# A feed-forward kernel in float32 halves: sums of weights spread over two steps, block 2 of the first layer in the order of blocks 0 and 1, and ScalarE's order at the turn of layers

## The chip, the cores and the metric

The kernel runs on one core of one Trainium2 chip. The metric is the device time of one execution in microseconds (us); a profiled execution gives the rows below. Engines are named as in the profile: PE (TensorE's matmuls), PEld (its weight loads), DVE (VectorE), ACT (ScalarE), POOL (GpSimd), SP (the queue that issues the transfers).

## The reference

Channel attention over 6016 tokens of 256 channels, and then two feed-forward layers of 2048 hidden columns, each with weights of its own:

```python
x = (v @ a).reshape(6016, 256)     # a: softmax of normalized k^T q, 256x256
h = x @ w_in                       # layer 1: 256 -> 2048
x = (h - np.tanh(h)) @ w_out       #          2048 -> 256
h = x @ w2_in                      # layer 2, the same sizes
g = np.where(h > 0.0, h, np.exp(np.minimum(h, 0.0)) - 1.0)
return g @ w2_out
```

The weights of both layers come as 64-bit numbers, which the kernel turns into float32 itself.

## The kernel before

**Products in halves.** Every operand of a matmul is split into a high and a low part (`ghi`/`glo`, `vhi`/`vlo`, `win` with `win_hi` and `win_lo`, `wout`), and a product is three matmuls: high by high, low by high, high by low. The split is a copy into the matmul's type on ACT (high) and a subtraction on DVE or POOL (low).

**Blocks and steps.** The tokens are cut into 12 blocks `b` of 512 columns (the last has 384), the hidden columns into 8 pairs of 128, `p`. The code counts layers from 0. A step `(layer, b, p)` makes `h` of one pair (12 matmuls of 512 columns into PSUM, `emit_h`, L270), applies the activation (ACT's tanh, DVE's `g = h - tanh`, ACT's `ghi`, the low part `glo`), and some steps later adds the pair's share of the output `o` (12 matmuls, `emit_out`, L869). `LAG` is that distance: `pend` holds the steps whose `o` is still to come.

**Seven products instead of eight.** From block 3 of the first layer on, odd steps with `p` in `PAIRS` = (1, 3, 5, 7) go through `emit_h7`: 21 matmuls of 256 columns (lines L672 to L674, PSUM tiles `q`), for which sums of the four weight blocks are needed (`wsum`, four tiles per pair and a high and low part) and sums of the four parts of the activations (`t`, `thi`, `tlo`, by `sum_v`). The results are put together on ACT and DVE into `hs` (L681 to L691).

**Sums of weights.** `own_sums(p)` makes `wsum` of the first layer: one addition of the two parts of `win` (`whole`, L627, 128x512), four sums of 128x128 (L612), a cast on ACT (L618), the low part (L619). Before, all of it but the cast is on POOL, and it is called after steps 1, 3, 5 and 7 of block 2. For the second layer `sums_of` runs in `conv.store()`, from two tiles `cut` of the converter, and writes to DRAM (`sums_dram`).

**The converter.** The class `Converter` turns the second layer's weights into parts in 32 units while the first layer runs. A unit passes through `load` (a transfer), `first` (two ACT instructions, L113 and L114), `second` (four DVE instructions, L130, L136, L142 and L149, which leave the tile `cut`), `third_scalar` (ACT, L190), `third_pool` (POOL, L197) and `store` (a transfer to DRAM). `nlow` and `ncut` are the numbers of buffers of two of its tiles; both are 3 for the late converter. Steps that go through `emit_h7` run no part of it. In block 11 the finished weights are loaded back over the first layer's.

**Order.** All of it is written out by hand, under a manual schedule, and each engine takes its instructions in that order. Blocks 0 and 1 run first, their steps interleaved, through `emit_act`, with `LAG` 2: tanh, `g`, the converter's parts, `ghi`, `glo`. All other blocks run through the class `Act` with `LAG` 3, in which `ghi` and `glo` of a step are issued in the step after:

```python
act = Act(layer, b, p, h[2][:, :, : blocks[b][1]])   # tanh, or exp and tanh
...
elif before and layer == 0:
    before.lower()                                   # glo of the step before
...
for fill in second:                                  # the converter on DVE
    fill()
conv.store()
...
act.begin()                                          # g = h - tanh
```

**PSUM.** Up to block 2, `h` has two buffers (pool `ps_h`). At block 3 this pool closes, `ps_q` opens in its place for the tiles `q`, and the `h` of even steps gets the one buffer of `ps_b`. So a `q` of block 3 cannot start before DVE has read both last `h` of block 2, and from then on each `h` waits for DVE's `g` of the even step before. `emit_evac` copies a finished `o` out of PSUM on ACT (`osb`, L886), after which the next block's `o` may start.

Of the kernel before, what the change touches and what calls it, by code (L numbers as in the profile page):

```python
# [8 lines left out]
F32 = mybir.dt.float32  # L9
# [3 lines left out]
ALU = mybir.AluOpType  # L13
# [9 lines left out]
def kernel(  # L23
# [488 lines left out]
    with tc.manual_schedule():  # L512
# [92 lines left out]
        def halves(x):  # L605
            return x.rearrange("p c (h t) -> p (c h) t", h=2)

        def sums_of(p, first, second, away):
# [25 lines left out]
        def sum_v(i, raw):  # L634

            x = halves(raw)
            t = steady[0].tile([P, 4, width // 2], F32, tag="t", name=f"t{i}")
            tt = nc.vector.tensor_tensor
            tt(out=t[:, 0:4:2], in0=x[:, 1:4:2], in1=x[:, 0:2], op=ALU.subtract)
            tt(out=t[:, 1], in0=x[:, 3], in1=t[:, 0], op=ALU.subtract)  # L640
            tt(out=t[:, 3], in0=x[:, 2], in1=t[:, 1], op=ALU.subtract)
            hi = steady[0].tile([P, 4, width // 2], F32R, tag="thi", name=f"thi{i}", bufs=2)
            nc.scalar.activation(out=hi, in_=t, func=AF.Copy)
            t_of[i] = (t, hi)
# [87 lines left out]

        def emit_act(layer, b, p, h, fold, late=False, full=False):
            _, n = blocks[b]
# [4 lines left out]
            def between():  # L739

                conv.third_scalar()
                conv.third_pool()
                conv.load()
                conv.first()


            second = conv.second()

# [26 lines left out]
            if layer == 0:  # L775
# [8 lines left out]
                between()  # L784
                nc.scalar.activation(out=hi, in_=g, func=AF.Copy)
            else:

# [133 lines left out]
        for s, (layer, b, p) in list(enumerate(order))[3 : 2 * NP]:  # L921
            if conv is early and early.done() and s >= starts[-1]:
                right.close()
                steady.append(ctx.enter_context(tc.tile_pool(name="steady", bufs=1, side="right")))
                wsum = steady[0].tile([P, 2, len(PAIRS), 4, P], F32R, name="wsum")
                conv = Converter(late_stack, "l", NU // 2, late_units, 3, 1, 3, 3)
                conv.load()
# [15 lines left out]
            if s == 2 * NP - 2:  # L943
                split_v(nv)
                nv += 1

        LAG = 3
        before = None
        for s, (layer, b, p) in list(enumerate(order))[2 * NP :]:
            if conv.done() and not conv.ready and not late_pool:  # L950
                late_stack.close()
# [39 lines left out]
            else:  # L991
                second = conv.second()
                if before and not before.apart and layer == 0:
                    before.upper()
                act = Act(layer, b, p, h[2][:, :, : blocks[b][1]])
                if before and before.apart:
                    before.begin()
                    before.end()
                    before.upper()
                    before.lower()  # L1000
                elif before and layer == 0:
                    before.lower()
                elif before:
                    before.upper()
                    before.lower()
                if done:
# [14 lines left out]
            if nv < len(phases):  # L1021
                if p == 0:
                    load_v(nv)
                    raw = v_of[nv]
                if p == 2:
                    split_v_scalar(nv)
                if p == 3:
                    split_v_rest(nv, nc.vector)
                apart = strassen(*phases[nv], PAIRS[0])
                if p == 5 and apart:  # L1030
                    sum_v(nv, raw)
                if p == 7:
                    if apart:
                        sum_v_rest(nv, nc.vector)
                    nv += 1
        before.upper()
# [40 lines left out]
```

## Time and profile before

| | us |
|---|---|
| median of 3 runs | 1056.19 (1054.81 to 1056.95) |
| the profiled execution | 1056.99 |
| its span, first to last instruction | 1055.0 |
| PE busy | 1024.9 (97%) |
| DVE busy | 883.0 (84%) |
| ACT busy | 680.7 (65%) |
| POOL busy | 284.7 (27%) |

A busy share is a mean over stages. The profile also has, for each engine, what an instruction waited for (the releaser) and how long, the busy times within any stretch of the span with TensorE's granted clock (1.00 is 2.4 GHz, 0.50 is 1.2 GHz), and the order in time. Times of rows count from the first instruction.

### The profile page before, as it was taken

The page shows a single profiled execution, that of the slowest core. Times are in us where ns is not written, and L with a number is a line of the kernel's source. Part 1 is how long each engine was busy: PE and PEld are TensorE (multiplying, and loading weights), DVE is VectorE, ACT ScalarE, POOL GpSimd, SP SyncE. Part 2 cuts the span into 40 slices and gives each one's busy share as a digit, 9 for nine tenths or more (in the row PEclk, how much of TensorE's full clock was granted, in tenths as well). Part 3 has the DMA queues.
Part 4 walks back from the last instruction along what each step waited for, and adds up shares of the span by engine and source line. Part 5 has one row for each costly group of instructions (what it writes and reads, how often), then busy time and mean ns, then how long its engine had stood idle before and what let it go on. Part 6 is the DMA issues. An engine that isn't in the chain of part 4 may idle for free.

```text
span 1055.0 us, 14543 instructions
## 1 busy us (share of the span) xinstructions
PE 1024.9 (97%) x5638; PEld 922.1 (87%) x5638; DVE 883.0 (84%) x1063; ACT 680.7 (65%) x850; POOL 284.7 (27%) x185
## 2 busy tenths in 40 slices
PE   9999997799999999999999999999999999999998
PEld 8888886689788798889999889989899899998998
DVE  7899978896979879777556889899889889889875
ACT  7887675565556565555544676766766667676664
POOL 4522225333323332322210212222122221221210
PEclk9999999899999999999999999999999999999999
DMA  9733123222223121110067100100100000000000
GB/s 357 271 100 100 51 80 110 90 91 80 90 70 97 64 90 51 71 51 16 21 218 225 52 21 21 40 21 21 41 21 21 24 37 21 21 28 28 21 10 27
DMA packets 49253, 75.65 MB, mean 72 GB/s; under 512 B 3360, under 2 KB 25120, under 8 KB 49184
## 3 DMA queue, kind: packets, MB, share of 16 engines
q1 hardware_dynamic: 48896, 74.20, 20.8%
q8 instruction: 44, 0.72, 0.3%
q10 hardware_dynamic: 288, 0.52, 0.1%
q14 instruction: 25, 0.20, 0.1%
HBM read 51.91 MB, written 22.81 MB: 71 GB/s over the span
## 4 chain that ended last, share of the span: by engine, by line
PE 71%; DVE 6%; ACT 3%; issue 1%; POOL 1%; DVEq 0%; ACTq 0%
PE o L869 35%; PE h L270 20%; PE q L673 5%; PE q L672 5%; PE q L674 5%; DVE g L716 2%; PE o_last L869 1%; DVE glo L729 1%; ACT osb L886 1%; ACT ghi L725 1%; POOL glo L729 1%; DVE vlo L250 1%; POOL sum L612 0%; DVE cut L142 0%; ACT vhi L243 0%
## 5 line engine op out<-in xcount | busy, mean ns | idle before, releaser
L869 PE MATMUL o<-ghi,wout 128*128 128x512 f32 (+1 forms) x1472 | 347.0, 379 | 2.5 <-ACT osb L886 2.4
L729 POOL TENSOR_TENSOR glo<-g,ghi 128x1024 fp32r<-128x1024 f32 x76 | 182.9, 2407 | 605.9 <-ACT ghi L725 482.1
L869 PEld LDWEIGHTS o<-ghi,wout 128*128 128x128 f32 x1472 | 272.0, 190 | 37.3 <-ACT osb L886 3.6
L270 PE MATMUL h<-vhi,win 128*128 128x512 f32 (+1 forms) x900 | 282.9, 376 | 14.8 <-DVE g L716 14.0
L725 ACT ACTIVATE ghi<-g 128x1024 fp32r<-128x1024 f32 (+1 forms) x175 | 182.4, 1042 | 87.1 <-DVE g L720 51.7
L270 PEld LDWEIGHTS h<-vhi,win 128*128 128x128 f32 x900 | 170.1, 190 | 41.0 <-DVE g L716 18.4
L869 PE MATMUL o<-glo,wout 128*128 128x512 f32 (+1 forms) x736 | 187.2, 377 | 0.0
L270 PE MATMUL h<-vlo,win 128*128 128x512 f32 (+1 forms) x450 | 168.5, 375 | 0.0
L869 PEld LDWEIGHTS o<-glo,wout 128*128 128x128 f32 x736 | 138.5, 189 | 18.9
L729 DVE TENSOR_TENSOR glo<-g,ghi 128x1024 fp32r<-128x1024 f32 (+1 forms) x99 | 119.0, 1202 | 36.6 <-ACT ghi L725 36.6
L712 DVE SCALAR_TENSOR_TENSOR g<-e,g 128x1024 f32<-128x1024 f32 (+1 forms) x95 | 114.2, 1202 | 23.5 <-ACT g L706 23.1
L270 PEld LDWEIGHTS h<-vlo,win 128*128 128x128 f32 x450 | 85.8, 191 | 10.6
L705 ACT ACTIVATE e<-hs 128x1024 f32<-128x1024 f32 x44 | 46.6, 1059 | 67.5 <-DVE hs L691 67.5
L684 DVE TENSOR_TENSOR hs<-q,hs 128x512 f32<-128x512 f32 x76 | 52.2, 687 | 38.0 <-ACT hs L681 30.1
L716 DVE TENSOR_TENSOR g<-h,g 128x1024 f32<-128x1024 f32 (+1 forms) x48 | 56.3, 1174 | 18.7 <-ACT g L702 18.7
L705 ACT ACTIVATE e<-h 128x1024 f32<-128x1024 f32 (+1 forms) x51 | 50.6, 992 | 32.7 <-PE h L270 32.6
L702 ACT ACTIVATE g<-h 128x1024 f32<-128x1024 f32 (+1 forms) x48 | 47.3, 985 | 34.7 <-PE h L270 33.9
L702 ACT ACTIVATE g<-hs 128x1024 f32<-128x1024 f32 x32 | 33.9, 1059 | 55.1 <-DVE hs L691 53.4
L720 DVE SCALAR_TENSOR_TENSOR g<-g,h 128x1024 f32<-128x1024 f32 (+1 forms) x51 | 60.4, 1185 | 5.7 <-DVE g L712 0.5
L673 PE MATMUL q<-tlo,wsum 128*128 128x256 f32 x228 | 63.2, 277 | 0.0
L672 PE MATMUL q<-thi,wsum 128*128 128x256 f32 x228 | 63.1, 277 | 0.0
L674 PE MATMUL q<-thi,wsum 128*128 128x256 f32 x228 | 63.0, 276 | 0.0
(179 smaller groups left out, 1753.6 us busy)
## 6 DMA issues: line engine op xcount, KB each, us to landing
qk<-in_q_dram SPq DMA_DIRECT2D x23, 256.0 KB, 5.0
vraw<-in_vT_dram SPq DMA_DIRECT2D x11, 512.0 KB, 4.0
x<-osb SPq DMA_DIRECT2D x11, 512.0 KB, 2.7
vraw<-x SPq DMA_DIRECT2D x11, 512.0 KB, 3.2
out_dram<-osb SPq DMA_DIRECT2D x11, 512.0 KB, 2.7
qk<-in_k_dram SPq DMA_DIRECT2D x21, 256.0 KB, 5.2
raw0in<-in_moe_w_in_dram SPq DMA_DIRECT2D x8, 512.0 KB, 3.8
raw0out<-in_moe_w_out_dram SPq DMA_DIRECT2D x8, 512.0 KB, 3.6
```

The lines of the kernel that those rows point to most:

```text
L270: nc.tensor.matmul(out=out, lhsT=w, rhs=x, start=(i == 0), stop=(i == len(pairs) - 1))
L672: nc.tensor.matmul(out=out, lhsT=weights[0], rhs=hi, start=first, stop=False)
L673: nc.tensor.matmul(out=out, lhsT=weights[0], rhs=lo, start=False, stop=False)
L674: nc.tensor.matmul(out=out, lhsT=weights[1], rhs=hi, start=False, stop=end)
L702: nc.scalar.activation(out=self.g, in_=h, func=AF.Tanh)
L705: nc.scalar.activation(out=self.e, in_=h, func=AF.Exp)
L712: nc.vector.scalar_tensor_tensor(out=self.g, in0=self.e, scalar=1.0, in1=self.g, op0=ALU.add, op1=ALU.mult)
L716: nc.vector.tensor_tensor(out=self.g, in0=self.h, in1=self.g, op=ALU.subtract)
L720: nc.vector.scalar_tensor_tensor(out=self.g, in0=self.g, scalar=0.0, in1=self.h, op0=ALU.min, op1=ALU.max)
L725: nc.scalar.activation(out=self.hi, in_=self.g, func=AF.Copy)
L729: engine.tensor_tensor(out=self.lo, in0=self.g, in1=self.hi.bitcast(F32), op=ALU.subtract)
L869: nc.tensor.matmul(out=columns(o[c][:, :n]), lhsT=w[:, f, c * P : (c + 1) * P], rhs=turned(x[:, i]), start=(f == 0 and w is wout_hi and x ...
```

## The change

Five things change:

- Block 2 of the first layer gets a loop of its own: `emit_act` and a `LAG` of 2, as for blocks 0 and 1. In it the converter runs in step 0 alone (`convert=p == 0`); its other seven units of that block move to later steps.
- `own_sums` runs on DVE, after steps 1, 2, 4 and 6. Its cast is issued behind the step's evacuation, and its low part in the next step (`sums_left`).
- For the second layer, POOL's four sums stay in `conv.store()`, and the cast, the low part and the transfer are issued in the converter's next step.
- The late converter has four buffers `cut` instead of three.
- At the turn of layers two ACT instructions change places: `ghi` of the last step of block 11 comes before the exp of the second layer's first step, and in step (1, 0, 2) the evacuation of block 11 comes before `ghi`.

```diff
-            sub = lambda o, a, b, op=ALU.subtract: nc.gpsimd.tensor_tensor(out=t[:, o], in0=a, in1=b, op=op)
+            engine = nc.gpsimd if away else nc.vector
+            sub = lambda o, a, b, op=ALU.subtract: engine.tensor_tensor(out=t[:, o], in0=a, in1=b, op=op)
...
-            nc.scalar.activation(out=dest[:, 0], in_=t, func=AF.Copy)
-            nc.gpsimd.tensor_tensor(out=dest[:, 1], in0=t, in1=dest[:, 0].bitcast(F32), op=ALU.subtract)
-            if away:
-                nc.sync.dma_start(out=sums_dram[j], in_=dest.bitcast(F32))
+            def cast():
+                nc.scalar.activation(out=dest[:, 0], in_=t, func=AF.Copy)
+
+            def low():
+                engine.tensor_tensor(out=dest[:, 1], in0=t, in1=dest[:, 0].bitcast(F32), op=ALU.subtract)
+                if away:
+                    nc.sync.dma_start(out=sums_dram[j], in_=dest.bitcast(F32))
+
+            sums_left.append((cast, low))
...
-            nc.gpsimd.tensor_tensor(
+            nc.vector.tensor_tensor(
                 out=a, in0=win_hi[:, :, fs].bitcast(F32), in1=win_lo[:, :, fs].bitcast(F32), op=ALU.add
...
                 nc.scalar.activation(out=hi, in_=g, func=AF.Copy)
+                for extra in work:
+                    extra()
...
-                conv = Converter(late_stack, "l", NU // 2, late_units, 3, 1, 3, 3)
+                conv = Converter(late_stack, "l", NU // 2, late_units, 3, 1, 3, 4)
...
+        OWN = (1, 2, 4, 6)
+        for s, (layer, b, p) in list(enumerate(order))[2 * NP : 3 * NP]:
+            h = emit_h(layer, b, p)
+            done = pend.pop(0)
+            emit_out(*done)
+            work = []
+            if p == 3:
+                work.append(lambda: split_v_rest(nv, nc.vector))
+            if p == 5:
+                work.append(lambda: sum_v(nv, raw_of[0]))
+            if p == 7:
+                work.append(lambda: sum_v_rest(nv, nc.vector))
+            if sums_left:
+                cast, low = sums_left.pop()
+                work.append(low)
+            if p in OWN:
+                work.append(lambda: own_sums(PAIRS[OWN.index(p)]))
+            pend.append((layer, b, p, emit_act(layer, b, p, h, None, convert=p == 0, work=work)))
+            emit_evac(*done[:3])
+            if sums_left:
+                sums_left[0][0]()
...
-        for s, (layer, b, p) in list(enumerate(order))[2 * NP :]:
+        for s, (layer, b, p) in list(enumerate(order))[3 * NP :]:
...
-                if before and not before.apart and layer == 0:
+                if before and not before.apart and before.layer == 0:
                     before.upper()
                 act = Act(layer, b, p, h[2][:, :, : blocks[b][1]])
                 if before and before.apart:
                     before.begin()
                     before.end()
+                    if (layer, b, p) == (1, 0, 2):
+                        emit_evac(*done[:3])
                     before.upper()
                     before.lower()
-                elif before and layer == 0:
+                elif before and before.layer == 0:
                     before.lower()
...
                 for fill in second:
                     fill()
+                if sums_left:
+                    for part in sums_left.pop():
+                        part()
                 conv.store()
...
-            if layer == 0 and b == 2 and p % 2 == 1:
-                own_sums(PAIRS[p // 2])
```

What else was at the end of the loop (loading and splitting the next block's input) became the function `prepare`, in the same order.

The first place is DVE in block 2 of the first layer, from step 4's `glo` of the step before to step 5's `g` (`h_2_4` is `h` of block 2, step 4; `hz` and `cut` are the converter's). Before:

```order
L729 TENSOR_TENSOR glo<-g,ghi 128x1024
L130 SCALAR_TENSOR_TENSOR hz<-sq,raw1in_1561 128x256
L136 TENSOR_SCALAR cut<-hz 128x256
L142 SCALAR_TENSOR_TENSOR cut<-hz,cut 128x256
L149 ISA cut<-cut,low 128x512
L716 TENSOR_TENSOR g<-h_2_4_1691,g 128x1024
```

In the change the same stretch, from step 4's `g` to step 5's, reads:

```order
L793 TENSOR_TENSOR g<-h_2_4_1657,g 128x1024
L636 TENSOR_TENSOR whole<-win 128x512
L615 TENSOR_TENSOR sum<-whole 128x128 x2
L615 TENSOR_TENSOR sum<-sum,whole 128x128
L615 TENSOR_TENSOR sum<-whole,sum 128x128
L770 TENSOR_TENSOR glo<-g,ghi 128x1024
L793 TENSOR_TENSOR g<-h_2_5_1697,g 128x1024
```

The four instructions of the converter ahead of `g` are gone, five of the sums stand behind `g`, and `glo` now belongs to the same step.

The second place is POOL in block 4, around the second layer's first sums of that block (`out` is the low part of a converted unit). Before:

```order
L729 TENSOR_TENSOR glo<-g,ghi 128x1024
L612 TENSOR_TENSOR sum<-cut 128x128 x2
L612 TENSOR_TENSOR sum<-sum,cut 128x128
L612 TENSOR_TENSOR sum<-cut,sum 128x128
L619 TENSOR_TENSOR sums_out<-sum,sums_out 128x512
L197 TENSOR_TENSOR out<-cut,out 128x256
```

In the change:

```order
L742 TENSOR_TENSOR glo<-g,ghi 128x1024
L615 TENSOR_TENSOR sum<-cut 128x128 x2
L615 TENSOR_TENSOR sum<-sum,cut 128x128
L615 TENSOR_TENSOR sum<-cut,sum 128x128
L197 TENSOR_TENSOR out<-cut,out 128x256
L742 TENSOR_TENSOR glo<-g,ghi 128x1024
L626 TENSOR_TENSOR sums_out<-sum,sums_out 128x512
```

The low part moved behind the `glo` of the converter's next step, and ACT's cast, which it waits for, moved with it.

The third place is ACT at the turn of layers, from the tanh of the last step of block 11 to the evacuation `osb` of that block. Before:

```order
L702 ACTIVATE g<-h_11_7_5345 128x2x384
L705 ACTIVATE e<-h_0_0_5385 128x1024
L706 ACTIVATE g<-h_0_0_5385 128x1024
L725 ACTIVATE ghi<-g 128x2x384
L681 ACTIVATE hs<-q_1_0_1_5423 128x256
L725 ACTIVATE ghi<-g 128x1024
L705 ACTIVATE e<-hs 128x1024
L706 ACTIVATE g<-hs 128x1024
L705 ACTIVATE e<-h_0_2_5475 128x1024
L706 ACTIVATE g<-h_0_2_5475 128x1024
L725 ACTIVATE ghi<-g 128x1024
L886 ACTIVATE osb<-o_11_5214 128x2x12x16 x2
```

In the change:

```order
L715 ACTIVATE g<-h_11_7_5345 128x2x384
L738 ACTIVATE ghi<-g 128x2x384
L718 ACTIVATE e<-h_0_0_5385 128x1024
L719 ACTIVATE g<-h_0_0_5385 128x1024
L694 ACTIVATE hs<-q_1_0_1_5423 128x256
L738 ACTIVATE ghi<-g 128x1024
L718 ACTIVATE e<-hs 128x1024
L719 ACTIVATE g<-hs 128x1024
L718 ACTIVATE e<-h_0_2_5475 128x1024
L719 ACTIVATE g<-h_0_2_5475 128x1024
L904 ACTIVATE osb<-o_11_5214 128x2x12x16 x2
L738 ACTIVATE ghi<-g 128x1024
```

The 384-column `ghi` moved ahead of the second layer's first exp, and `osb` ahead of the last `ghi` shown.

## Rows read from the trace of the kernel before

**Rows 1.** Waits of PE from 100 us on: total us, times, longest.

```profile
PE h L270 <- DVE g L716: 14.0, 9, 2.4
PE q L672 <- DVE g L716: 6.0, 1, 6.0
PE o L869 <- ACT osb L886: 2.4, 1, 2.4
```

**Rows 2.** Windows by block: us; busy (count) PE, PEld, DVE, ACT, POOL; clock; DMA.

```profile
139.54:185.78 46.24, 39.92 (x182) 33.70 (x180) 34.08 (x45) 28.41 (x43) 20.74 (x28) 1.00 0.34 109
185.78:234.63 48.85, 42.85 (x229) 38.06 (x228) 44.83 (x61) 30.09 (x46) 18.34 (x16) 0.93 0.29 92
234.63:279.47 44.84, 42.42 (x229) 37.70 (x228) 33.56 (x49) 26.01 (x37) 15.39 (x13) 0.96 0.25 83
279.47:320.40 40.93, 40.73 (x230) 36.52 (x229) 33.83 (x47) 25.43 (x36) 11.82 (x7) 1.00 0.24 77
320.40:365.71 45.31, 42.85 (x229) 37.66 (x228) 39.42 (x52) 26.21 (x38) 16.60 (x15) 0.96 0.26 82
...
406.64:450.28 43.64, 41.18 (x230) 36.51 (x228) 37.13 (x47) 24.76 (x34) 15.63 (x14) 1.00 0.18 61
450.28:490.74 40.46, 40.46 (x230) 36.60 (x228) 29.29 (x37) 22.48 (x25) 10.48 (x6) 1.00 0.14 43
...
564.66:607.60 42.94, 40.57 (x230) 36.79 (x230) 34.38 (x40) 25.90 (x30) 7.23 (x3) 0.96 0.30 97
```

**Rows 3.** The chain that ended last, one piece: start us, us.

```profile
244.91 2.59 PE h L270 x12
```

**Rows 4.** Timeline at the end of block 2 and in block 3: start us, us.

```profile
180.60 0.63 ACT L618 ACTIVATE wsum<-sum 128x512 fp32r<-128x512 f32 x1 [3.05 <-POOL sum L612]
197.09 0.58 PE L672 MATMUL q<-vhi,win 128*128 128x256 f32 x1 [5.97 <-DVE g L716]
```

**Rows 5.** Timeline in block 4, step 4: DVE, ACT, PE.

```profile
264.72 0.53 DVE L136 TENSOR_SCALAR cut<-hz 128x256 uint32<-128x256 uint32 x1 [4.03 <-POOL sum L612]
265.67 0.63 ACT L618 ACTIVATE sums_out<-sum 128x512 fp32r<-128x512 f32 x1 [4.24 <-POOL sum L612]
267.56 0.48 PE L270 MATMUL h<-vhi,win 128*128 128x512 f32 x1 [2.42 <-DVE g L716]
```

**Rows 6.** Timeline in block 5: DVE twice, POOL once.

```profile
306.35 2.64 DVE L149 CUSTOM_DVE_ANT_0 cut<-cut,low 128x512 uint16<-128x512 uint16 x1
317.56 0.42 DVE L149 CUSTOM_DVE_ANT_0 cut<-cut,low 128x512 uint16<-128x512 uint16 x1
306.33 2.37 POOL L729 TENSOR_TENSOR glo<-g,ghi 128x1024 fp32r<-128x1024 f32 x1 [8.31 <-ACT ghi L725]
```

**Rows 7.** Timeline at the turn of layers: ACT three times, PE once.

```profile
569.27 0.84 ACT L725 ACTIVATE ghi<-g 128x768 fp32r<-128x768 f32 x1
580.61 1.06 ACT L725 ACTIVATE ghi<-g 128x1024 fp32r<-128x1024 f32 x1 [0.72 <-DVE g L720]
581.58 1.51 ACT L886 ACTIVATE osb<-o 128x384 f32<-128x384 f32 x2
583.14 3.52 PE L869 MATMUL o<-ghi,wout 128*128 128x512 f32 x8 [2.37 <-ACT osb L886]
```

**Rows 8.** Groups of instructions by line: busy us, mean ns, idle before.

```profile
L729 DVE TENSOR_TENSOR glo<-g,ghi 128x1024 fp32r<-128x1024 f32 x84 | 103.3, 1230 | 12.4 <-ACT ghi L725 12.4
L716 DVE TENSOR_TENSOR g<-h,g 128x1024 f32<-128x1024 f32 x40 | 48.7, 1218 | 14.1 <-ACT g L702 14.1
L639 DVE TENSOR_TENSOR t<-vraw 128x512 f32<-128x512 f32 x19 | 13.1, 688 | 0.0
L640 DVE TENSOR_TENSOR t<-vraw,t 128x256 f32<-128x256 f32 x19 | 8.1, 425 | 0.7
L627 POOL TENSOR_TENSOR whole<-win 128x512 f32<-128x512 f32 x4 | 5.2, 1304 | 0.0
L612 POOL TENSOR_TENSOR sum<-whole 128x128 f32<-128x128 f32 x8 | 4.2, 546 | 0.3
```

More of the change, by code (lines that the diff above doesn't have):

```diff
@@ L606, in halves @@
             return x.rearrange("p c (h t) -> p (c h) t", h=2)
+        sums_left = []
         def sums_of(p, first, second, away):
@@ L641, in sum_v, with sum_v_scalar @@
             tt(out=t[:, 3], in0=x[:, 2], in1=t[:, 1], op=ALU.subtract)
+            t_of[i] = t
+        def sum_v_scalar(i):
+            t = t_of[i]
             hi = steady[0].tile([P, 4, width // 2], F32R, tag="thi", name=f"thi{i}", bufs=2)
@@ L731, with emit_act @@
         lower = []
-        def emit_act(layer, b, p, h, fold, late=False, full=False):
+        def emit_act(layer, b, p, h, fold, late=False, full=False, convert=True, work=()):
             _, n = blocks[b]
@@ L739, in between @@
             def between():
+                if not convert:
+                    return
+                conv.store()
                 conv.third_scalar()
@@ L744, in between @@
                 conv.first()
-            second = conv.second()
+            second = conv.second() if convert else []
             def fill(i):
@@ L945, with prepare @@
                 nv += 1
+        def prepare(p):
+            nonlocal nv
+            if nv == len(phases):
+                return
+            apart = strassen(*phases[nv], PAIRS[0])
+            if p == 0:
+                load_v(nv)
+                raw_of[0] = v_of[nv]
+            if p == 2:
+                split_v_scalar(nv)
+            if p == 3:
+                split_v_rest(nv, nc.vector)
+            if p == 5 and apart:
+                sum_v(nv, raw_of[0])
+                sum_v_scalar(nv)
+            if p == 7:
+                if apart:
+                    sum_v_rest(nv, nc.vector)
+                nv += 1
+        raw_of = [None]
+        OWN = (1, 2, 4, 6)
[4 more added lines that the diff above has]
+            work = []
+            if p == 3:
+                work.append(lambda: split_v_rest(nv, nc.vector))
+            if p == 5:
+                work.append(lambda: sum_v(nv, raw_of[0]))
+            if p == 7:
+                work.append(lambda: sum_v_rest(nv, nc.vector))
[8 more added lines that the diff above has]
+                sums_left[0][0]()
+            if p == 0:
+                load_v(nv)
+                raw_of[0] = v_of[nv]
+            if p == 2:
+                split_v_scalar(nv)
+            if p == 5:
+                sum_v_scalar(nv)
+            if p == 7:
+                nv += 1
         LAG = 3
         before = None
-        for s, (layer, b, p) in list(enumerate(order))[2 * NP :]:
-            if conv.done() and not conv.ready and not late_pool:
+        for s, (layer, b, p) in list(enumerate(order))[3 * NP :]:
+            if conv.done() and not conv.ready and not sums_left and not late_pool:
                 late_stack.close()
@@ L1005 @@
                     before.lower()
-                if done:
+                if done and (layer, b, p) != (1, 0, 2):
                     emit_evac(*done[:3])
@@ L1018 @@
             pend.append((layer, b, p, (act.hi, act.lo)))
-            if layer == 0 and b == 2 and p % 2 == 1:
-                own_sums(PAIRS[p // 2])
[L1021 to L1035, printed above, removed]
+            prepare(p)
         before.upper()
```

## The prediction

> **What bounds the kernel now.** The page comes first: PE is busy for 97% of the span, so time can only be won where PE waits or runs at the lower clock. Next comes the list of PE's waits behind the attention part [rows 1]: 14.0 us in nine waits of `h` for DVE's `g`, 6.0 us in one wait of `q` for the same, and 2.4 us in one wait of `o` for ACT's `osb`. The windows by block show where they lie and what they cost in all [rows 2]. A block in which PE never waits takes 40.46 us (block 9, and block 10 is the same to 0.01 us): eight `o`, four `h` and four `q`. One `h` or one `o` is 12 matmuls and takes 2.59 us [rows 3].
>
> So block 2, eight `h` and seven `o` in its window, would take 15 x 2.59 = 38.85 us and takes 46.24: 7.39 lost. Against 40.46, block 3 loses 8.39, block 4 4.38, block 5 0.47, block 6 4.85, block 7 again 0.47 (its row is like block 5's), block 8 3.18. Together 29.13 us. The first block of the second layer has three `o` of 384 columns in place of 512, so its floor is 40.46 - 3 x 2.59 x 0.25 = 38.52 us; it takes 42.94 and loses 4.42. That is more than the 22.4 us of waits: the granted clock's mean is 0.93 in block 3 and 0.96 in blocks 4, 6 and the turn, so a part of each ran at 1.2 in place of 2.4 GHz, behind a pause of 2.4 us or more [rows 2, 4, 5, 7]. Block 8 has the pause and a clock of 1.00, and loses some 1.2 to 1.7 us less than blocks 4 and 6: a fall does not follow each such pause.
>
> **Block 2 and the way into block 3.** Before, DVE computes `g` behind the converter's four instructions, and ACT stands in front of `wsum`'s cast until POOL has made the sums: 3.05 us for the third pair, and much the same for the other three [rows 4]. Tanh, `g`, `ghi` and `glo` of a step hang on one another, the delay adds up from step to step, and at the end `q` finds the last `h` unread: 5.97 us [rows 4].
>
> The change takes seven units of the converter out of this block and POOL's work too. What DVE gets for it: for each pair one `whole` of 128x512, four sums of 128x128, one low part of 128x512, spread over two steps. A DVE instruction of 128x512 takes 0.69 us, one of 128x256 0.43 [rows 8]; one of 128x128 is not shown on DVE. Bounds: 0.21 (half of the 256-column one) and 0.55 (POOL's own 128x128 sum); I take 0.30, nearer DVE's row, since part of an instruction is fixed: from 512 to 256 columns only 0.26 of 0.69 goes. Two steps, 4 and 5, the fullest: two `g` and two `glo`, 2 x (1.22 + 1.23) = 4.90; sums 0.69 + 1.20 + 0.69 = 2.58; the three instructions for `t`, 0.69 + 2 x 0.43 = 1.55. Sum 9.03 us, in the 10.36 us that PE needs for two steps of 5.18. At POOL's prices (1.30, 4 x 0.55, 1.30) it would be 11.2 and cost at most 0.9 us in each of four pairs, 3.5 us in all; I take nothing, and keep 3.5 for the range.
>
> The waits that are added: the cast stands on ACT behind `g` and the sums, and the next tanh behind it. In steps 1 and 2, with the two `osb` or `vhi` on ACT as well, I expect a tanh 1 to 2 us late. It is covered: `h` has two buffers, so the `h` two steps on starts 3 x 2.59 = 7.77 us after this one's end, and tanh and `g` need some 2.3. `glo` now stands behind the sums on DVE; with a `LAG` of 2 its `o` comes four pieces, 10.36 us, after the end of `h`, and the chain up to `glo` is about 6. The first `q` of block 3 starts one `o` and one `h`, 5.18 us, behind the last `h` of block 2, and tanh and `g` of that step are done after about 2.3. So block 2 should run at PE's pace, and both of its losses go, 7.39 and nearly all of block 3's 8.39.
>
> **The second layer's sums.** In block 4 DVE's L136 waits 4.03 us for POOL's sums, which free the tile `cut` that it writes, ACT's cast waits 4.24 us for them, and PE's next `h` 2.42 [rows 5]. It happens three times: in blocks 4, 6 and 8. With the fourth `cut` the sums that a unit has to await are those of the converter's step before, about 10 us old; the cast and the low part come another step later and find their inputs ready. These waits go.
>
> What stays is what blocks 5 and 7 show, 0.47 us each. There L149 takes 2.64 us in place of 0.42, from the start of POOL's `glo` to its end [rows 6]: DVE stands still beside POOL, `g` is late, and `h` with it. The seven units that left block 2 now run in blocks 8 to 10, four to a block, so blocks 9 and 10 get this loss too. I put 0.47 on blocks 3, 5, 7 and 9, and 0.7 on blocks 4, 6, 8 and 10, which have the sums on top (block 4 lost nothing before its sum; the cast is 0.63 us of ACT): 4.7 us. Bounds: nothing, and twice 0.47 in all eight blocks, 7.5.
>
> The Trainium skill (SBUF — State Buffer, section "SBUF: two separate sides") says that VectorE and GpSimd share a port pair which one instruction holds alone, and that the other "fully blocks". The 2.64 beside 2.37 us agrees. It speaks against this change as far as converter steps move to blocks that had none: were the whole block of 2.2 us to reach PE in the seven moved steps, they would cost 15.5 us where the rows of blocks 5 and 7 say 0.12 a step, 0.8.
>
> **The turn of layers.** `o` of the second layer waits 2.37 us for block 11's evacuation, which takes 1.51 us and stands behind a `ghi` that itself waited 0.72 us [rows 7]. Put ahead of that `ghi`, with nothing else moved, it would run from 579.89 to 581.40 and end 1.69 us sooner: 0.7 of the wait would be left. The 384-column `ghi` of 0.84 us, which stood between the second layer's first tanh and the next `hs`, moves to where ACT was idle, and DVE's `glo` behind it; that takes most of the rest. I take 0.1 left and no fall of the clock: 4.3 of 4.42. Bounds: 1.7 (only the step above) and 4.4. The `ghi` now behind `osb` is wanted by an `o` two pieces later, over 5 us, which covers 1.5.
>
> **Sum.** 29.13 - 4.7 + 4.3 = 28.7 us. The profiled execution took 1056.99 us (1055.0 from first to last instruction, 2.0 around it), 0.8 over the median of 1056.19. So 1028.3 by the one and 1027.5 by the other: I say **1028 us**.
>
> **Rivals.**
> The sums go on stalling: the cast or L136 still waits for POOL, only elsewhere. For it: POOL's order keeps `glo`, of 2.4 us, ahead of the sums. Against: a whole converter step now lies between. Blocks 4, 6 and 8 lose 11.0 over what block 5 loses, 3.7 each; in four blocks 14.7 in place of the 0.9 put there: 1042 us.
>
> DVE goes on setting block 2's pace. For it: the sums are new work on DVE, and ACT's cast waits for DVE in the same step. Against: 9.0 of 10.36 us. With 7.4 kept, 1035; with block 3's wait kept as well, 1043.
>
> The turn keeps its wait, since something else, such as `hs`, is what makes `osb` late: 1028 + 4.3 = 1032 us.
>
> Slower: the standstill of DVE beside POOL reaches PE. Place: L149 in the 32 converter steps of blocks 3 to 10. Price: up to 2.22 us each. What the change can win without these steps is 29.13 + 4.3 = 33.4 us, so it decides from 1.04 us a step on; at the full price 71 us come in and 33.4 go out, 1094 us. For it: `glo` and L149 start together [rows 6], and the sums follow on POOL. Against: in blocks 5 and 7 the same standstill left 0.12 us a step, since the `h` that waits for `g` has an `o`, a `q` and an `o` before it.
>
> **How the numbers follow.** Forecast 0.64 (its own range 1024 to 1032, from the bounds of the residue and of the turn); the turn kept 0.12; the sums stall 0.10; DVE paces block 2 0.11, half of it on either side of 1037; slower 0.03. Below, no more can go than all 33.5: 1022.6. The range from 1023 to 1037 leaves out the stalling sums, half of the DVE case and the slower one, 0.18. A measurement of this kernel tells 0.2%, 2 us, from no change; all cases but the last are well past it, and 0.01 is left for no change: faster 0.96, same 0.01, slower 0.03.
>
> **What would show it.** In the profile after, the list of PE's waits should have no wait over 1 us between 100 us and the turn, none of `q` for `g`, and none or a short one of `o` for `osb`. The window of block 2 should be 8 x 5.18 = 41.4 us, the next one, with one `o` less, 38 to 38.5, blocks 4 to 10 between 40.5 and 41.4, and the clock 1.00 in all. L136 and the casts should wait for no sum; L149 should still have calls of 2.6 us, now up to block 10. I am wrong if block 2 takes over 43 us, if an even block takes over 42, or if blocks 9 and 10 show a new wait of PE.

## The result, and the profile after

The changed kernel takes 1027.49 us (median of 4 runs, 1027.16 to 1029.13) against 1055.5 of the kernel before in the same set of runs; the ratio is 0.974, 95% interval [0.9718, 0.9761]. In a second set of runs, on another chip, it took 1029.70 and the kernel before 1055.12: 0.9762 [0.9745, 0.9778]. The forecast was 1028. The profiled execution took 1027.36 us, its span is 1025.6 (before 1055.0), PE is busy for 99% of it, and the granted clock is 1.00 throughout.

The waits of PE from 100 us on, in the changed kernel (line, releaser: us in total, times, longest):

```profile
PE h L270 <- DVE g L729: 1.4, 7, 0.2
PE o L887 <- ACT osb L911: 0.2, 1, 0.2
```

Of the 22.4 us in [rows 1] 1.6 are left, and no wait is over 0.21 us. The windows by block, which answer to [rows 2] (us; busy PE, PEld, DVE, ACT, POOL; clock; DMA): blocks 2, 3, 4, 5, 9 and 10, and the first two blocks of the second layer.

```profile
139.59:181.03 41.44, 41.44 (x193) 36.29 (x192) 32.78 (x52) 26.25 (x32) 0.74 (x1) 1.00 0.17 58
181.03:219.38 38.35, 38.16 (x218) 34.26 (x217) 32.85 (x46) 24.39 (x35) 9.30 (x6) 1.00 0.24 76
219.38:260.79 41.41, 41.17 (x229) 36.51 (x228) 39.50 (x49) 26.13 (x38) 15.79 (x14) 1.00 0.27 90
260.79:301.72 40.93, 40.72 (x229) 36.52 (x228) 35.19 (x49) 25.61 (x37) 12.80 (x9) 1.00 0.24 77
...
424.52:465.46 40.94, 40.73 (x230) 36.52 (x229) 35.19 (x49) 25.62 (x37) 12.81 (x9) 1.00 0.22 71
465.46:505.92 40.46, 40.46 (x230) 36.60 (x229) 31.72 (x42) 23.45 (x31) 16.85 (x14) 1.00 0.18 62
539.36:577.90 38.54, 38.54 (x230) 35.65 (x229) 33.00 (x38) 25.90 (x30) 7.24 (x3) 1.00 0.33 110
577.90:618.81 40.91, 40.73 (x229) 36.67 (x228) 37.08 (x43) 27.68 (x32) 9.57 (x4) 1.00 0.07 27
```

The sixteen pieces of block 2 take 16 x 2.59 us and PE never stops in them. Block 3 has no wait of `q` any more. Blocks 6, 7 and 8 (left out) are 40.93 to 40.94 as block 5 is, where they had been 45.31, 40.93 and 43.64. The last row shows a new loss: the second layer's second block took 40.45 before (607.60 to 648.05) and now takes 40.91.

The window of the two fullest steps of block 2 on DVE, from one `g` to the `g` two steps on:

```profile
164.31:174.58 10.27, 8.35 (x14) 1.00 0.01 2
```

DVE is busy for 8.35 of 10.27 us. The price that was missing, a sum of 128x128 on DVE, and the casts on ACT in that block (busy us and mean ns of the group; then start and us of the rows, with the wait and its releaser in brackets):

```profile
L615 DVE TENSOR_TENSOR sum<-whole 128x128 f32<-128x128 f32 x8 | 2.0, 288 | 0.1
```

```profile
157.77 0.63 ACT L623 ACTIVATE wsum<-sum 128x512 fp32r<-128x512 f32 x1 [1.20 <-DVE sum L615]
158.31 1.05 ACT L243 ACTIVATE vhi<-vraw 128x1024 fp32r<-128x1024 f32 x1
159.26 1.01 ACT L792 ACTIVATE g<-h 128x1024 f32<-128x1024 f32 x1
163.16 1.02 ACT L792 ACTIVATE g<-h 128x1024 f32<-128x1024 f32 x1 [0.55 <-PE h L270]
```

The cast waits 1.20 us at most, in place of 3.05. At PE's pace of 5.18 us a step, counted back from the tanh at 163.16, the tanh behind this cast and `vhi` would start at 157.98; it starts at 159.26, 1.3 us late, and the one behind the cast before it 0.4 us late. The tanh at 163.16 already waits for PE again, so the delay is used up within a step.

The second layer's sums in block 4 of the changed kernel, which answer to [rows 5] (timeline of all engines, rows of ACT, POOL, DVE and PE):

```profile
246.55 0.61 ACT L623 ACTIVATE sums_out<-sum 128x512 fp32r<-128x512 f32 x1
...
246.73 2.38 POOL L742 TENSOR_TENSOR glo<-g,ghi 128x1024 fp32r<-128x1024 f32 x1 [6.12 <-ACT ghi L738]
246.80 2.58 DVE L149 CUSTOM_DVE_ANT_0 cut<-cut,low 128x512 uint16<-128x512 uint16 x1
249.06 1.46 POOL L626 TENSOR_TENSOR sums_out<-sum,sums_out 128x512 fp32r<-128x512 f32 x1
249.31 1.21 DVE L729 TENSOR_TENSOR g<-h,g 128x1024 f32<-128x1024 f32 x1
...
250.57 0.48 PE L270 MATMUL h<-vhi,win 128*128 128x512 f32 x1 [0.21 <-DVE g L729]
```

The cast waits for nothing. What is late here is `g`, and it is late by L149, which began 0.07 us behind POOL's `glo` and ended 0.27 us behind it: 2.58 us in place of 0.42. The wait of PE that it leaves is 0.21 us, but the block loses 0.47 by it: from `h` to `h` PE needs 10.12 us, this one starts 10.48 behind the one at 240.09, and its first matmul takes 0.48 us in place of 0.38. The other 0.48 us of block 4 is lost in its first steps, where an `o` starts late behind the evacuation `osb` (the weight load of that `o`):

```profile
237.39 1.59 PEld L887 LDWEIGHTS o<-ghi,wout 128*128 128x128 f32 x8 [0.22 <-ACT osb L904]
```

Two calls of L149 stood ahead of it, at 225.73 and 235.61 (2.65 and 2.61 us).

The turn of layers, on ACT:

```profile
551.98 1.01 ACT L719 ACTIVATE g<-h 128x1024 f32<-128x1024 f32 x1
552.94 1.58 ACT L904 ACTIVATE osb<-o 128x384 f32<-128x384 f32 x2
554.28 1.10 ACT L738 ACTIVATE ghi<-g 128x1024 fp32r<-128x1024 f32 x1
```

The evacuation starts right behind the tanh ahead of it, is over at 554.52, and the `o` that needs it starts at 555.08 without a wait; [rows 7] had 2.37.

### The profile page after: what moved, and what is told of

It reads as the page before. It is cut to its first block, busy times and chain, and to the rows that moved or that the text cites. A ratio compares the mean times of both kernels' runs of the same rounds, so it can differ in the third digit from the quotient of the medians.

```text
span 1025.6 us, 14532 instructions
## 1 busy us (share of the span) xinstructions
PE 1016.4 (99%) x5638; PEld 917.7 (89%) x5638; DVE 883.5 (86%) x1087; ACT 680.5 (66%) x850; POOL 266.6 (26%) x161
## 4 chain that ended last, share of the span: by engine, by line
PE 82%; DVE 10%; ACT 4%; issue 3%; DVEq 0%; ACTq 0%
PE o L887 38%; PE h L270 24%; PE q L687 4%; PE q L686 4%; PE q L685 4%; PE S L338 4%; DVE g L729 2%; PE o_last L887 1%; ACT osb L904 1%; DVE glo L742 1%; DVE vlo L250 1%; PE aw L270 1%; DVE hs L700 1%; DVE hs L697 1%; DVE g L725 1%
## 5 line engine op out<-in xcount | busy, mean ns | idle before, releaser
L738 ACT ACTIVATE ghi<-g 128x1024 fp32r<-128x1024 f32 (+1 forms) x167 | 173.8, 1041 | 99.2 <-DVE g L733 51.4
L742 DVE TENSOR_TENSOR glo<-g,ghi 128x1024 fp32r<-128x1024 f32 (+1 forms) x91 | 108.0, 1187 | 20.1 <-ACT ghi L738 20.1
L270 PEld LDWEIGHTS h<-vlo,win 128*128 128x128 f32 x450 | 85.1, 189 | 10.3
L697 DVE TENSOR_TENSOR hs<-q,hs 128x512 f32<-128x512 f32 x76 | 52.1, 686 | 40.7 <-ACT hs L694 39.3
L700 DVE TENSOR_TENSOR hs<-q,hs 128x512 f32<-128x512 f32 x76 | 52.6, 692 | 8.3 <-DVE hs L697 0.5
L733 DVE SCALAR_TENSOR_TENSOR g<-g,hs 128x1024 f32<-128x1024 f32 x44 | 53.9, 1225 | 1.5
```

The lines of the kernel that those rows point to most:

```text
L270: nc.tensor.matmul(out=out, lhsT=w, rhs=x, start=(i == 0), stop=(i == len(pairs) - 1))
L697: tt(out=hs[:, 0:8:4], in0=quads(q62), in1=two(3), op=ALU.add)
L700: tt(out=hs[:, 1:3], in0=quads(q57), in1=two(0), op=ALU.add)
L733: nc.vector.scalar_tensor_tensor(out=self.g, in0=self.g, scalar=0.0, in1=self.h, op0=ALU.min, op1=ALU.max)
L738: nc.scalar.activation(out=self.hi, in_=self.g, func=AF.Copy)
L742: engine.tensor_tensor(out=self.lo, in0=self.g, in1=self.hi.bitcast(F32), op=ALU.subtract)
```

## The experiments

Windows of all kernels, each from the start of the same `h` to the start of the same `h`, in us (the profiled execution of each; c1 is the first block of the second layer, and 40.46 is a block without a wait, for c1 38.52; the median is that of all runs of a kernel):

| | 2 | 3 | 4 | 5 | 6 | 7 | 8 | 9 | 10 | c1 | median, us |
|---|---|---|---|---|---|---|---|---|---|---|---|
| before | 46.24 | 48.85 | 44.84 | 40.93 | 45.31 | 40.93 | 43.64 | 40.46 | 40.46 | 42.94 | |
| fourth `cut` | 46.28 | 50.50 | 43.01 | 41.04 | 43.36 | 41.04 | 41.57 | 40.57 | 40.46 | 42.98 | 1053.11 |
| sums spread | 46.18 | 49.37 | 45.72 | 40.46 | 45.26 | 40.93 | 44.96 | 40.46 | 40.46 | 41.40 | 1058.49 |
| both | 46.26 | 50.07 | 41.36 | 41.95 | 40.93 | 41.97 | 41.26 | 40.46 | 40.46 | 41.40 | 1048.84 |
| turn alone | 46.25 | 49.34 | 45.33 | 40.92 | 43.63 | 41.56 | 44.84 | 40.46 | 40.46 | 38.54 | 1051.97 |
| block 2 alone | 41.44 | 38.35 | 44.34 | 40.94 | 43.24 | 41.68 | 44.39 | 41.41 | 42.58 | 41.40 | 1042.44 |
| idle converter | 38.85 | 40.93 | 44.36 | 41.39 | 44.35 | 40.94 | 43.24 | 40.92 | 41.38 | 43.09 | 1041.23 |
| changed | 41.44 | 38.35 | 41.41 | 40.93 | 40.94 | 40.93 | 40.93 | 40.94 | 40.46 | 38.54 | 1027.49 |

The first four ran beside a kernel before of 1055.88, the two on block 2 beside 1056.33. Where block 2 ends one `o` earlier (the order of before), its floor is 38.85 and that of block 3 is 40.46.

**The second layer's sums: a fourth buffer alone.**

```diff
-                conv = Converter(late_stack, "l", NU // 2, late_units, 3, 1, 3, 3)
+                conv = Converter(late_stack, "l", NU // 2, late_units, 3, 1, 3, 4)
```

> The kernel before with a fourth buffer `cut` and nothing else. My theory: the loss of blocks 4, 6 and 8 (12.4 us together) has two stalls side by side, DVE's L136 for the free `cut` (4.03 us) and ACT's cast for POOL's sums (4.24 us), and each alone makes `g` late by as much. Then this run takes only DVE's stall away, the tanh behind the cast stays late, and the time falls by 0 to 3 us, to 1053 to 1056. Rival: DVE's stall is what reaches PE, since L136 stands ahead of `g`; then blocks 4, 6 and 8 come down to about 41 us and the time falls by 10 to 11 us, to 1045.

1053.11 us, ratio 0.9971 [0.9961, 0.9981]: 0.3% less, which is what I expected of it, but blocks 4, 6 and 8 each come down by 1.8 to 2.1 us, so the two stalls do not simply stand in for each other, as I had put it. Block 4 in the timeline (ACT, PE):

```profile
268.13 0.63 ACT L618 ACTIVATE sums_out<-sum 128x512 fp32r<-128x512 f32 x1 [4.44 <-POOL sum L612]
...
279.44 0.48 PE L270 MATMUL h<-vhi,win 128*128 128x512 f32 x1 [1.46 <-DVE g L716]
```

L136 waits no longer. ACT's cast does, for 4.44 us, and the wait of PE that it leaves comes only at the next `h`, 11 us later, and is 1.46 us, with the clock at 1.00 in blocks 4, 6 and 8. Not all of it shows in the time, since block 3 took 1.65 us more in the profiled execution, with the clock's mean at 0.90 behind the wait of `q` that this kernel keeps.

**The spread alone.**

```diff
-            nc.scalar.activation(out=dest[:, 0], in_=t, func=AF.Copy)
-            nc.gpsimd.tensor_tensor(out=dest[:, 1], in0=t, in1=dest[:, 0].bitcast(F32), op=ALU.subtract)
-            if away:
-                nc.sync.dma_start(out=sums_dram[j], in_=dest.bitcast(F32))
+            def rest():
+                nc.scalar.activation(out=dest[:, 0], in_=t, func=AF.Copy)
...
+                sums_left.append(rest)
```

> The kernel before; from block 3 on the cast, the low part and the transfer of the second layer's sums come in the converter's next step, with three buffers `cut` as before. My theory (each stall alone is enough): ACT's 4.24 us for the sums go, DVE's wait in L136 for the free `cut` stays, and the time falls by 0 to 3 us. Rival: ACT's cast is what reaches PE, through the tanh behind it; then the time falls by 10 to 11 us, to 1045.

1058.49 us, ratio 1.003 [1.0019, 1.0041]: slower than the kernel before, which neither side expected. DVE and PE in block 4:

```profile
266.25 0.53 DVE L136 TENSOR_SCALAR cut<-hz 128x256 uint32<-128x256 uint32 x1 [4.05 <-POOL sum L615]
...
269.50 0.48 PE L270 MATMUL h<-vhi,win 128*128 128x512 f32 x1 [2.85 <-DVE g L726]
```

With three buffers L136 waits as before, and PE's wait is 2.85 us in place of 2.42. So DVE's wait is the one that stops PE at once; the cast is a second, smaller one behind it.

**Both.**

> The kernel before with both: four buffers `cut`, and the sums spread over two steps from block 3 on. Forecast by the prediction's terms: blocks 4, 6 and 8 lose about 0.7 each in place of 4.38, 4.85 and 3.18, so 10.3 us less, 1045 us; blocks 2 and 3 and the turn keep their losses. Rival (the sums go on stalling elsewhere, since POOL's `glo` still stands ahead of them): 1053 to 1056.

1048.84 us, ratio 0.9939 [0.9922, 0.9956]: 7.0 us less, more than the sum of the two parts (2.8 less and 2.6 more), but not the 10.3 expected. Blocks 4, 6 and 8 lost 12.41 and now lose 0.90, 0.47 and 0.80, 10.2 less, as forecast. Blocks 5 and 7 give 1.0 us back each, and block 3, which keeps its wait of `q`, 1.2. The group of L149 in this kernel, from 235 to 443 us (busy us, mean ns), and in the kernel before, from 234 to 450:

```profile
L149 DVE CUSTOM_DVE_ANT_0 cut<-cut,low 128x512 uint16<-128x512 uint16 x19 | 34.5, 1813 | 0.7
```

```profile
L149 DVE CUSTOM_DVE_ANT_0 cut<-cut,low 128x512 uint16<-128x512 uint16 x19 | 21.3, 1121 | 0.7
```

The 19 calls take 13 us more: twelve of them stand in place of six. That the steps now meet POOL's `glo` at other times is how I read it. In block 5 three of four stand, and `h` waits there (1.49 lost in place of 0.47). In the changed kernel the converter's units lie elsewhere, and nine of the 30 calls stand (20 us above 0.42 each, at 2.2 us).

**The turn alone.**

```diff
-                if before and not before.apart and layer == 0:
+                if before and not before.apart and before.layer == 0:
+                    if (layer, b, p) == (1, 0, 2):
+                        emit_evac(*done[:3])
```

> The kernel before with the two places of ACT at the turn of layers alone: the 384-column `ghi` ahead of the second layer's first exp, and block 11's evacuation ahead of `ghi` in step (1, 0, 2). By the prediction's term 4.3 us less, 1051 us; PE's wait of `o` for `osb` falls from 2.4 to under 0.3 us. Rival (something else makes `osb` late): within 1 us of the kernel before, with the wait still about 2 us.

1051.97 us, 3.9 less, ratio 0.9967 [0.9956, 0.9978]; c1 falls by 4.40 to 38.54, and PE waits for `osb` nowhere.

**One edit of the turn at a time**, taken out of the changed kernel.

> The changed kernel without the first edit at the turn: the 384-column `ghi` of block 11's last step stands behind the second layer's first exp and tanh again, as before; the evacuation stays ahead of `ghi` in step (1, 0, 2). By the prediction's step 0.7 us of PE's wait for `osb` is left: 0.5 to 0.9 us above the changed kernel. Rival (the evacuation's place gives all of it): no difference, wait 0.

> The changed kernel without the second edit at the turn: the evacuation of block 11 behind `ghi` of step (1, 0, 2) again; the 384-column `ghi` stays moved. By the prediction's step the evacuation is 1.7 us later than in the changed kernel (1.06 of `ghi` and up to 0.72 of its wait), less what the moved `ghi` of 0.84 gives back: PE waits 0.9 to 1.7 us for `osb`, and the time is 0.9 to 1.7 us above the changed kernel. Rival (this edit is worth nearly all of 4.4, a fall of the clock included): 2.5 to 4.4 us above it.

Beside the changed kernel at 1029.70 us they took 1030.66 and 1029.98 (1027.31 to 1031.24); these times alone tell neither from nothing. The timelines do; first the kernel with the 384-column `ghi` at its old place, then the one with the evacuation at its old place:

```profile
558.28 1.99 PE L887 MATMUL o<-ghi,wout 128*128 128x512 f32 x8 [0.62 <-ACT osb L904]
```

```profile
558.48 1.99 PE L887 MATMUL o<-ghi,wout 128*128 128x512 f32 x8 [1.01 <-ACT osb L904]
```

c1 takes 39.66 and 39.82. Either edit by itself shortens the wait from 2.37 to 1.01 or less, with the clock at 1.00 in both, and both are needed for the last 1.1 to 1.3 us. Of the 4.4 us, 1.5 are the clock's and not safely the edits': in three kernels with the order of before at the turn (sums spread, both, block 2 alone) PE waits 2.4 us for `osb` as before, the clock is 1.00 all the same, and c1 takes 41.40. The last of them:

```profile
551.33:592.73 41.40, 39.04 (x229) 35.69 (x229) 33.52 (x39) 25.75 (x30) 7.26 (x3) 1.00 0.28 98
```

From there to 38.54 it is 2.9 us.

**Block 2's loop alone.** The loop, the own sums on DVE and the converter in step 0 only are as in the change; the second layer's sums stay in one step, with three `cut`, and the turn is as before.

> Block 2's own loop alone (LAG 2, converter in step 0 only, own sums on DVE); the second layer's sums stay in one step, three buffers `cut`, ACT's order at the turn as before. By the prediction's terms the 7.4 us of block 2 and some 7.9 of block 3 go; the seven units that move to blocks 8 to 10 bring a fourth sum, in block 10, at 3.7 us, and some 0.9 of residue: 10.7 us less in all, 1045 us. Block 2 should take 41.4 us in place of 46.2, with no wait of `q`. Rival (DVE goes on setting block 2's pace): block 2 at 45 to 46 us, and the time within 3 us of the kernel before, or above it.

1042.44 us, ratio 0.9869 [0.9846, 0.9893], 13.9 less, where 10.7 was expected. Block 2 takes 41.44 and `q` waits for nothing; so much was forecast. The fourth sum is there (block 10: 42.58), but costs 2.1 us in place of 3.7: block 10 has one wait of 1.41 us. Blocks 4, 6 and 8 have two each, 0.65 to 1.60 us where there had been one of 2.4, and still lose 2.8 to 3.9; the clock stays at 1.00 behind all of them. Another 1.5 us of the gain is c1 at 1.00 in place of 0.96, which no edit of this kernel touches.

**The idle converter.** One part of that: the converter does nothing in steps 1 to 7 of block 2. The sums stay on POOL, the loop is that of the class `Act`, `LAG` is 3.

```diff
-                second = conv.second()
+                works = b != 2 or p == 0
+                second = conv.second() if works else []
...
-                conv.store()
-                conv.third_scalar()
-                conv.third_pool()
-                conv.load()
-                conv.first()
+                if works:
+                    conv.store()
...
```

> The kernel before, with the converter idle in steps 1 to 7 of block 2 (its units move to later blocks) and nothing else: the own sums stay on POOL, the order is that of the class Act, LAG 3. It asks which part of block 2's change frees it. Theory A, the converter is the cause: without its four DVE instructions ahead of `g` and without POOL's work for it, block 2 comes down to 41.4 to 43 us and the wait of `q` goes; with a fourth sum in block 10 (3.7 us) and 0.9 of residue that makes about 1045 to 1047. Theory B, the sums on POOL and the cast on ACT that waits for them are the cause: block 2 stays above 45 us, the wait of `q` stays above 4 us, and the time is 1056 to 1060. In between (each takes a part): block 2 at 43 to 45.

1041.23 us, ratio 0.9868 [0.9846, 0.9891]: below what theory A had set, and as much as the whole new loop gives. The windows of blocks 2 and 3:

```profile
139.53:178.38 38.85, 38.85 (x182) 34.02 (x181) 27.82 (x28) 25.21 (x31) 21.51 (x25) 1.00 0.18 62
178.38:219.31 40.93, 40.72 (x230) 36.52 (x228) 33.97 (x46) 24.61 (x35) 10.53 (x7) 1.00 0.22 71
```

Together 79.78 us, and 79.79 in the changed kernel. A cast of these sums on ACT:

```profile
157.26 0.62 ACT L618 ACTIVATE wsum<-sum 128x512 fp32r<-128x512 f32 x1
```

It waits for nothing, though POOL makes the sums as before: what made it wait 3.05 us [rows 4] was the converter's work. Theory A holds and B falls. The converter's instructions on DVE and those on POOL and ACT went together here; which of them counts is not shown.

**The own sums back on POOL**, in the changed kernel.

```diff
-            engine = nc.gpsimd if away else nc.vector
+            engine = nc.gpsimd
...
-            nc.vector.tensor_tensor(
+            nc.gpsimd.tensor_tensor(
```

> The changed kernel with the first layer's own sums back on POOL, at the same places in the program, the cast and the low part still apart. If it is the place of the sums, not the engine, that counts: block 2 keeps 41.4 us and the time stays within 1 us of the changed kernel, 1026.5 to 1029; POOL has nothing else in this block, and the cast's wait for `sum` grows to some 3 to 4 us, which the five us of slack of tanh cover. Rival (the engine counts: POOL's slower sums make the tanh behind the cast late beyond its slack): 1030 to 1036, with waits of `h` for `g` in block 2.

1029.51 us, ratio 0.9755 [0.9735, 0.9774], 0.5 over the range that I had set but inside what the changed kernel shows (0.974 and 0.9762); blocks 2 and 3 take 41.44 and 38.34, and a cast waits 2.26 us at most, not 3 to 4. The engine of the sums decides nothing.

**What is left, first try.** The changed kernel once more as the base, and a kernel that issues the converter's four DVE instructions ahead of `before.begin()` (the `g` of `hs`).

> The changed kernel again, as the base for the three runs beside it: 1026.5 to 1028.5 us.

> The changed kernel, with the converter's four DVE instructions of a step issued ahead of the putting together of `hs` of the step before, in place of behind it. What is left of losses in blocks 3 to 9 of the changed kernel is 3.8 us, 0.47 to 0.95 a block, and in each the late `h` follows an L149 that lasted 2.6 us beside POOL's `glo`. Theory: this standstill is all that is left; ahead of `hs` L149 runs when POOL has no `glo`, takes 0.42 us, and the time falls by 2.5 to 3.8 us, to about 1024. Rival: DVE's 2.5 us for the four instructions now stand ahead of `hs` and make tanh and `g` of the odd steps late instead; then the time is the same or up to 8 us more.

The base took 1029.70 us, 1.2 over the top of what I had set. The trial took 1038.43, ratio 0.9843 [0.9827, 0.986]: 8.7 us worse, so the rival holds. L149 is short there in all 30 calls (425 ns in the mean), but ACT's `ghi` now waits for the later `g`, the evacuation stands behind `ghi`, and PE waits for it (ACT, then PE, in block 5):

```profile
278.86 1.06 ACT L738 ACTIVATE ghi<-g 128x1024 fp32r<-128x1024 f32 x1 [1.70 <-DVE g L729]
279.82 1.89 ACT L904 ACTIVATE osb<-o 128x512 f32<-128x512 f32 x2
```

```profile
281.76 3.64 PE L887 MATMUL o<-ghi,wout 128*128 128x512 f32 x8 [2.35 <-ACT osb L904]
```

Four such waits make 8.6 us, and blocks 5, 7 and 9 take 44.7 us.

**What is left, second try.** Only L149 moves: it is held back to the next step, behind `hs` and ahead of `glo`.

```diff
-                for fill in second:
+                for fill in second[:3]:
                     fill()
+                held.extend(second[3:])
...
             if seven:
+                while held:
+                    held.pop()()
                 before.upper()
                 before.lower()
```

> The changed kernel; from block 3 on the converter's fourth DVE instruction, L149, is held back to the next step, behind `hs` and ahead of `glo`, and the other three stay where they are. In the changed kernel L149 starts beside POOL's `glo` and stands up to 2.6 us in place of 0.42, with `g` of the even step behind it. Theory: this is what is left of losses in blocks 3 to 9, some 3.8 to 4.7 us; at its new place POOL's `glo` is done, L149 takes 0.42 us in most calls, `g` comes no later than without a standstill, and the blocks fall to 40.46 us (block 4 too): 2.5 to 4.5 us below the changed kernel, a ratio to the kernel before of 0.970 to 0.973 where the changed kernel has 0.974 to 0.976. Rival: at the new place it delays `hs`, `glo` or the other products and PE waits there, or POOL's low parts make it stand as long; then the ratio is 0.975 or more.

1023.57 us (1023.13 to 1024.04), ratio 0.9698 [0.9685, 0.9712], where the changed kernel has 0.974 and 0.9762: faster than both kernels, and the theory holds. Its list of PE's waits from 100 us on has one line, its windows of blocks 3 and 4 are the floors, and blocks 5 to 10 take 40.46 each:

```profile
PE o L887 <- ACT osb L911: 0.2, 1, 0.2
```

```profile
181.10:218.97 37.87, 37.87 (x217) 34.33 (x216) 31.41 (x48) 24.29 (x35) 10.01 (x7) 1.00 0.23 77
218.97:259.43 40.46, 40.46 (x229) 36.60 (x228) 32.17 (x48) 26.03 (x37) 14.98 (x13) 1.00 0.27 92
```

L149 in blocks 3 to 10, in the changed kernel and in this one (busy us, mean ns):

```profile
L149 DVE CUSTOM_DVE_ANT_0 cut<-cut,low 128x512 uint16<-128x512 uint16 x30 | 32.5, 1083 | 1.0
```

```profile
L149 DVE CUSTOM_DVE_ANT_0 cut<-cut,low 128x512 uint16<-128x512 uint16 x30 | 12.5, 415 | 0.0
```

20 us of standstill on DVE were 3.8 us on PE (spans 1025.6 and 1021.8).

This kernel also takes 0.42 us of work from ahead of `g`, so it might be that and not the standstill. The second profile of the changed kernel tells them apart, in block 5, where L149 keeps its place and happens not to stand (DVE, PE):

```profile
288.41 0.42 DVE L149 CUSTOM_DVE_ANT_0 cut<-cut,low 128x512 uint16<-128x512 uint16 x1
288.75 1.22 DVE L729 TENSOR_TENSOR g<-h,g 128x1024 f32<-128x1024 f32 x1
291.88 0.38 PE L270 MATMUL h<-vhi,win 128*128 128x512 f32 x1
```

The `h` waits for nothing and starts 10.12 us behind the one before it.

## Why the prediction was right, step by step

**Blocks 2 and 3**, 7.39 + 8.39 to go: block 2 lost nothing, and block 3 loses 38.35 - 37.87 = 0.48, which is the residue put there. The cause was named too broadly. I gave the credit to two things together, the converter's units and POOL's work for the sums; the idle converter shows that the units alone account for it, and the sums on POOL show that their move to DVE gives nothing. The change had both, so its time could not tell them apart. The price of a 128x128 sum (0.30, measured 0.288) was right; the load of the two fullest steps (9.03, measured 8.35 of 10.27) was some 8% too high, and no term of the sum hung on it. The tanh behind the casts of steps 1 and 2 are late by 0.4 and 1.3 us, where the text had 1 to 2, and covered, as it said.

**Blocks 4, 6 and 8**, the sums: L136 and the cast wait no longer; the two halves of the edit are both needed, as the fourth buffer and the spread alone show. That a stall of the cast costs less than one of L136 was not in the text.

**The residue**, 4.7 with bounds of 0 and 7.5: measured 0.48 + 0.95 + 5 x 0.47 + 0 = 3.8 us. It is, as said, L149's standstill beside `glo`: with it gone the blocks lie on their floors. The split was off. Even blocks with a sum were to lose more than odd ones; 6 and 8 lose the same 0.47, and block 10 nothing. It is not a constant of a block, nor of the kernel: the second profile has 40.92 in block 10 and loses 4.7 us in blocks 3 to 10. L149 from 180 to 506 us in that profile, and in the kernel with the evacuation at its old place, which loses 6.1 us there:

```profile
L149 DVE CUSTOM_DVE_ANT_0 cut<-cut,low 128x512 uint16<-128x512 uint16 x30 | 43.5, 1448 | 1.0
L149 DVE CUSTOM_DVE_ANT_0 cut<-cut,low 128x512 uint16<-128x512 uint16 x30 | 54.5, 1815 | 1.0
```

So 9, 14 and 19 standing calls go with 3.8, 4.7 and 6.1 us. In the two profiles of the changed kernel the places fit as well: a block loses 0.46 to 0.48 where its third call stands (`h` is late), and as much where its first two stand (`o` is). That the sum of this term came out near 4.7 has a part of luck, since which calls stand was not in the text.

**The turn**, 4.3: 4.40 measured, in the changed kernel and alone. The 0.7 us that the evacuation's move would leave by itself came out as a wait of 0.62. Of the 4.40, 1.5 is the clock at 0.96 in the profile of before; three kernels with the old turn have 41.40 at 1.00, so 2.9 is what the edits are sure to give. New, and not in the text, is the 0.46 us in the block behind it, where `o` waits 0.2 us for `osb`.

**Sum.** 29.13 - 3.8 + 4.40 - 0.46 = 29.3 us, against 28.7 forecast; the profiled execution went from 1056.99 to 1027.36, 29.6 less. The forecast's own range was not added up right: residues of 0 and 7.5 with turns of 4.4 and 1.7 make some 1023 to 1033, not 1024 to 1032.

**The signs.** Of the three signs of being wrong, the last came for one of its two blocks: block 9 took 40.46 before and takes 40.94, with a new wait of PE of 0.21 us. The sign contradicted the text's own residue of 0.47 for that block, so it was badly chosen; the mechanism behind it is the one forecast.

**The rivals.** The stalling sums, DVE's pace in block 2 and the turn's wait show nowhere in the changed kernel. The slower case had the right mechanism and too high a price: 3.8 us over the 30 calls of L149 in blocks 3 to 10 (the text had 32 steps) are 0.13 each, near what blocks 5 and 7 had shown, and it would have decided from 1.04.

## What to carry to other kernels

An engine that runs ahead of its consumer on average can still stop PE where its queue puts background work ahead of the one result that PE needs next: here leaving seven background units out of block 2, with the loop as it was, was worth as much as the rewritten loop. Where two stalls end at nearly the same time, take one away at a time and then both: one half alone won 2.8 us, the other lost 2.6, both won 7.0. And read the short instructions whose duration varies between calls: a mean of 1083 ns where the single call takes 0.42 us was the whole of what was left in blocks 3 to 10.

## What the runs showed of the hardware

The standstill of DVE goes by who starts first. In the changed kernel both of these started at 308.08 (POOL, DVE):

```profile
308.08 2.67 POOL L742 TENSOR_TENSOR glo<-g,ghi 128x1024 fp32r<-128x1024 f32 x1 [5.41 <-ACT ghi L738]
308.08 0.42 DVE L149 CUSTOM_DVE_ANT_0 cut<-cut,low 128x512 uint16<-128x512 uint16 x1
```

Here L149 took its 0.42 us and POOL's `glo` 2.67 in place of 2.38; at 246.80, 0.07 us behind `glo`, L149 took 2.58. In the changed kernel all nine calls that started 0.01 to 0.08 us behind a `glo` stood, and in all six that started with one `glo` took 2.67. So a difference of less than 0.1 us decides over 2.2 us of DVE, which fits that the losses move between blocks from version to version. The Trainium skill (SBUF — State Buffer, section "SBUF: two separate sides") says the same: of the two, the one that starts first has the port pair that they share for its whole instruction. These runs agree, in both directions (2.58 in place of 0.42, and 2.67 in place of 2.38). The instructions of DVE here that read one input from PSUM did not stand: `hs<-q` (L697) took 0.67 to 0.69 us in all 76 calls, 58 of which started while `glo` ran. In the last kernel L149 stands behind them.

A wait of 2.2 to 2.9 us was followed by a stretch at the lower clock, 1.2 GHz, in some blocks and not in others: the window's mean is 0.96 in blocks 4 and 6 of the kernel before and 1.00 in blocks 2 and 8, each with a wait of about 2.4 us. In blocks 2 to 10 and c1 of these profiles the clock was 1.00 wherever no wait was over 1.81 us.
